# Seven block products in place of eight for the first product of layer 2, with that layer's weights staged through DRAM

## The chip, the cores and the metric

The program runs on one core of one Trainium2 chip. The metric is the device time of one execution in microseconds (us), as the median of three runs.

## The reference

Attention for 4 batches of 8 heads gives 2304 rows of 512. Two feed-forward layers follow, each with two matrix products around an activation:

```python
q_s, k_s = softmax(q, axis=-1), softmax(k, axis=2)      # 4 x 8 x 576 x 64
x = (q_s @ (k_s.T @ v)) laid out as 2304 x 512
h = x @ w_in1                   # 2304 x 2048
x = silu(h) @ w_out1            # 2304 x 512
h = x @ w_in2                   # 2304 x 2048
out = (h * tanh(softplus(h))) @ w_out2     # "mish"
```

All inputs and the output are float32.

## The kernel before, in words

Every float32 operand of the feed-forward products is split into a high part of TensorE's `float32r` type and a low part, the remainder. A product is then three products: high by high, high by low, low by high. The split costs a copy on ScalarE and a subtraction on VectorE. Before that, a weight is "decoded" (`w_take`, `w_join`), which is an activation on ScalarE and two or three bit operations on VectorE.

Activations lie transposed, 512 features in 4 groups of 128 partitions (`KC = 4`) by 2304 tokens. The 2048 hidden features are 16 chunks of 128 (`NCH = 16`). Each layer makes two passes (`passes`, p = 0 to 3) over 8 chunks each (`HALF = 8`). Pass 0 takes the tokens in six blocks of 384 (`NARROW`), the others in five blocks of 512, 512, 256, 512 and 512 (`WIDE`).

The order within a pass is the list `events`. `X` splits a token block. `G1` (`ev_g1`) makes one chunk of h: 12 matmuls of 128 by 128 weights with a token block as the moving side, into one PSUM bank, then the activation on ScalarE, and a cast and a subtraction on VectorE that split the result g. `G2` (`ev_g2`) is the second product with that chunk, three chunks later (`SKEW = 3`): 12 matmuls into four banks in layer 1, and in layer 2 three matmuls for each 128 tokens, with g as the stationary side and 512 columns of weights as the moving side. `E` (`ev_e`) adds up or copies out the four banks.

Pass 0 is woven with the attention, in an order that a scheduler makes from priorities. From the event where the attention's work is used up, all engines follow the written order: `InOrder` (line 49; calls before that are recorded at line 47). There the pools of the first part are closed and others are opened in the same memory, and `w_plan` sets the decoding of each later weight chunk at a time counted in events. A pass's 16 weight pieces are fetched from DRAM (`w_dma`, lines 156 and 161, three staging buffers `st`), decoded into `wt` and split into resident tiles (`w_high`, `w_low`) during the pass before it.

Of the kernel before, what the change touches and what calls it, by code (L numbers as in the profile page):

```python
# [7 lines left out]
F32 = mybir.dt.float32  # L8
# [24 lines left out]

class InOrder:
# [21 lines left out]
def attention_silu_mish(ctx: ExitStack, tc: tile.TileContext, q, k, v, w_in1, w_out1, w_in2, w_out2, out):  # L56
    nc = tc.nc
    SP = nc.sync
    V, S, G, T = (InOrder(tc, e) for e in (nc.vector, nc.scalar, nc.gpsimd, nc.tensor))
# [19 lines left out]
    PARTS = (((0, HALF), (HALF, NCH)),) * 2  # L79
# [21 lines left out]
    wres = ctx.enter_context(tc.tile_pool(name="wres", bufs=HALF))  # L101
# [6 lines left out]
    xa = xp.tile([P, KC * NT], F32, name="xa")  # L108
# [15 lines left out]

    passes = [(L, c0, c1) for L in range(2) for c0, c1 in PARTS[L]]
    blocks = [NARROW] + [WIDE] * (len(passes) - 1)
    events, need = [], []
    for p, (L, c0, c1) in enumerate(passes):
        cs = list(range(c0, c1))
        pend = []  # L130
        for j in range(len(blocks[p])):
            events.append(("X", p, j, 0))
            for c in cs:
                events.append(("G1", p, j, c))
                pend.append(("G2", p, j, c))
                if len(pend) > SKEW:
                    events.append(pend.pop(0))
            events.extend(pend)
            pend = []
# [10 lines left out]
    def w_dma():  # L150
        kind, p, _, c = need[state["dma"]]
        state["dma"] += 1
        L = passes[p][0]
# [12 lines left out]
    def at(i):  # L166

        tc.cur_priority = 10000 + int(1000 * i)

# [9 lines left out]
    def w_decode():  # L179
# [14 lines left out]
        w = wres.tile([P, 2, 512], F32R, tag="wi" if kind == "G1" else "wo", name="w")  # L194
# [23 lines left out]
    def w_plan(start):  # L218
        first_mish = next(i for i, e in enumerate(events) if e[1] == len(PARTS[0]))
        ends, taken, split = [], start, 0.0  # L220
        for n in range(N0, len(need)):
            kind, p, _, c = need[n]
            last = max(i for i, e in enumerate(events) if e == (kind, p - 1, len(blocks[p - 1]) - 1, c - HALF if c >= HALF else c + HALF))
            if n % N0 == 0:
                taken = max(taken, nat[("X", p - 1, 1, 0)])
# [6 lines left out]
            signed = b < first_mish - 1  # L232
            box = {}
            for k, f in ((b, w_take), (b + 1.0, w_join), (s, w_high), (s + 1.0, w_low)):
                todo.setdefault(int(k), []).append((k, f, n, signed, box))

    def w_take(n, signed, box):
# [4 lines left out]
        tf, hi = t.bitcast(F32), st[:, 1].bitcast(F32)  # L242
        if signed:
            S.activation(out=tf, in_=hi, func=ACTF.Prelu, scale=W_BIAS, alpha=W_SIGN)
            V.tensor_scalar(out=st[:, 0], in0=st[:, 0], scalar1=29, scalar2=None, op0=ALU.logical_shift_right)
        else:
            S.mul(tf, hi, W_BIAS)

    def w_join(n, signed, box):
        st, t = box["st"], box["t"]  # L250
        lo, hi = st[:, 0], st[:, 1]
        if signed:
            V.scalar_tensor_tensor(out=t, in0=t, scalar=3, in1=lo, op0=ALU.logical_shift_left, op1=ALU.bitwise_or)
        else:
            V.tensor_scalar(out=t, in0=t, scalar1=3, scalar2=None, op0=ALU.logical_shift_left)
            V.scalar_tensor_tensor(out=t, in0=hi, scalar=0x80000000, in1=t, op0=ALU.bitwise_and, op1=ALU.bitwise_or)
            V.scalar_tensor_tensor(out=t, in0=lo, scalar=29, in1=t, op0=ALU.logical_shift_right, op1=ALU.bitwise_or)

    def w_high(n, signed, box):
        kind, p, _, c = need[n]  # L260
        wt[(kind, p, c)] = w = wres.tile([P, 2, 512], F32R, tag="wi" if kind == "G1" else "wo", name="w")
        S.copy(w[:, 0], box["t"].bitcast(F32))

    def w_low(n, signed, box):
        kind, p, _, c = need[n]
        w = wt[(kind, p, c)]
# [558 lines left out]
```

## Time and profile before

| | before |
|---|---|
| median of 3 runs | 880.09 us (879.54 to 880.23) |
| the profiled execution: its time | 879.92 us |
| its span | 878.1 us |
| TensorE matmul (PE) busy | 860.3 us, 98% of the span |
| VectorE (DVE) busy | 437.2 us, 50% |
| ScalarE (ACT) busy | 296.7 us, 34% |
| moved by DMA | 53.17 MB, of it 4.72 MB written to HBM |

The span is what the profile covers; 1.8 us of the execution's time lie outside it. PE is the stream of matmuls, PEld the loads of stationary operands, which overlap it. A busy share does not tell what sets the end: for that the rows below show the chain of waits and stretches in order of time.

### The profile page before, as it was taken

What the parts mean: (1) busy time and instruction counts of PE and PEld (TensorE: products, weight loads), DVE (VectorE), ACT (ScalarE), POOL (GpSimd) and SP (SyncE); (2) the same over time, 40 slices, a digit from 0 to 9 for tenths busy, and PEclk for the clock granted to TensorE, in tenths of its full rate; (3) what the DMA queues carried; (4) which work ended last, traced back from release to release, by engine and by line L of the source; (5) the groups of instructions that cost most, each with busy time, mean ns of one, the idle gap of its engine ahead of it and who ended that gap; (6) DMA issues with size and microseconds to landing.
All of it is one profiled execution on the core that took longest, in us unless ns stands there. A gap on an engine that the chain in (4) does not pass through costs nothing.

```text
span 878.1 us, 11558 instructions
## 1 busy us (share of the span) xinstructions
PE 860.3 (98%) x4618; PEld 744.0 (85%) x4618; DVE 437.2 (50%) x904; ACT 296.7 (34%) x553; POOL 54.4 (6%) x82
## 2 busy tenths in 40 slices
PE   7899999999989999999999999999999999999998
PEld 6688989999989888898888888888888888888886
DVE  4999366773267634352357424463268433333332
ACT  5887254573155312121144222231144111121110
POOL 3145111231000000000000000000000000000000
PEclk9999999999999999999999999999999999999999
DMA  9996211310034401120013001130012010100101
GB/s 237 246 228 142 74 37 37 73 37 1 1 119 130 134 1 49 49 97 1 0 49 120 25 1 48 49 96 1 1 48 72 1 39 10 46 27 1 43 6 48
DMA packets 61909, 53.17 MB, mean 61 GB/s; under 512 B 30368, under 2 KB 55456, under 8 KB 61856
## 3 DMA queue, kind: packets, MB, share of 16 engines
q1 hardware_dynamic: 61856, 52.44, 21.3%
q8 instruction: 36, 0.59, 0.3%
q14 instruction: 17, 0.14, 0.1%
HBM read 47.71 MB, written 4.72 MB: 60 GB/s over the span
## 4 chain that ended last, share of the span: by engine, by line
PE 89%; DVE 5%; ACT 1%; DMA 1%; issue 1%; ACTq 0%; DVEq 0%; SPq 0%
PE psum L49 72%; PE psum L47 17%; DMA st<-in_moe_w_out_dram 1%; DVE g L47 1%; DVE qz L47 1%; DVE kmx L47 1%; DVE w L47 0%; DMA st<-in_moe_w_in_dram 0%; ACT xa L47 0%; DVE st L47 0%; DVE wt L47 0%; DVE xs L47 0%; DVE qmx L47 0%; DVE xs L49 0%; ACT xs L49 0%
## 5 line engine op out<-in xcount | busy, mean ns | idle before, releaser
L49 PE MATMUL psum<-xs,w 128*128 128x512 f32 (+2 forms) x1548 | 327.9, 366 | 1.8 <-ACT gf L49 1.8
L49 PEld LDWEIGHTS psum<-xs,w 128*128 128x128 f32 x1548 | 271.3, 189 | 47.7 <-ACT gf L49 2.1
L49 ACT ACTIVATE gf<-psum 128x512 f32<-128x512 f32 (+2 forms) x129 | 71.0, 550 | 407.5 <-PE psum L49 292.1
L49 PE MATMUL psum<-w,g 128*128 128x512 f32 x864 | 204.3, 390 | 0.0
L49 PEld LDWEIGHTS psum<-w,g 128*128 128x128 f32 x864 | 161.7, 188 | 33.0
L49 DVE CAST g<-gf 128x512 fp32r<-128x512 f32 (+2 forms) x129 | 51.3, 397 | 277.0 <-ACT gf L49 267.8
L49 PE MATMUL psum<-g,w 128*128 128x512 f32 (+2 forms) x624 | 128.8, 361 | 0.5 <-DVE g L49 0.5
L49 PEld LDWEIGHTS psum<-g,w 128*128 128x128 f32 x624 | 109.0, 188 | 15.8 <-DVE g L49 0.8
L47 PE MATMUL psum<-xs,w 128*128 128x384 f32 x468 | 98.4, 350 | 2.9 <-ACT gf L47 2.1
L47 PEld LDWEIGHTS psum<-xs,w 128*128 128x128 f32 x468 | 80.3, 189 | 7.1 <-ACT gf L47 3.2
L47 PE MATMUL psum<-g,w 128*128 128x384 f32 x432 | 84.7, 343 | 1.3 <-DVE g L47 1.3
L49 DVE TENSOR_TENSOR g<-gf,g 128x512 fp32r<-128x512 f32 (+2 forms) x129 | 81.7, 633 | 4.4
L47 PEld LDWEIGHTS psum<-g,w 128*128 128x128 f32 x432 | 74.7, 188 | 2.6 <-DVE g L47 1.8
L49 ACT CAST w<-wt 128x512 fp32r<-128x512 f32 x48 | 29.6, 617 | 23.0 <-DVE wt L49 14.6
L47 DVE CAST g<-gf 128x384 fp32r<-128x384 f32 x39 | 16.1, 413 | 38.9 <-ACT gf L47 38.6
L49 ACT ACTIVATE wt<-st 128x512 f32<-128x512 f32 x48 | 32.1, 670 | 4.5 <-DMA st<-in_moe_w_in_dram 4.5
L49 DVE TENSOR_TENSOR w<-wt,w 128x512 fp32r<-128x512 f32 x48 | 32.6, 685 | 0.5 <-ACT w L49 0.3
L47 ACT ACTIVATE gf<-psum 128x384 f32<-128x384 f32 x39 | 18.9, 490 | 40.9 <-PE psum L47 36.9
L47 ACT ACT_TABLE_LOAD x22 | 28.2, 1283 | 4.3 <-PE psum L47 2.4
L47 DVE TENSOR_TENSOR g<-gf,g 128x384 fp32r<-128x384 f32 x39 | 25.1, 644 | 1.0
L49 DVE TENSOR_TENSOR xa<-psum,xa 128x512 f32<-128x512 f32 x18 | 11.5, 686 | 27.5 <-PE psum L49 27.5
L49 DVE SCALAR_TENSOR_TENSOR wt<-st,wt 128x512 uint32<-128x512 uint32 x34 | 23.5, 692 | 1.2
(108 smaller groups left out, 546.7 us busy)
## 6 DMA issues: line engine op xcount, KB each, us to landing
st<-in_moe_w_in_dram SPq DMA_DIRECT2D x32, 512.0 KB, 3.8
st<-in_moe_w_out_dram SPq DMA_DIRECT2D x32, 512.0 KB, 3.4
out_dram<-xa SPq DMA_DIRECT2D x18, 256.0 KB, 2.1
xb<-in_k_dram SPq DMA_DIRECT2D x16, 144.0 KB, 3.4
xb<-in_v_dram SPq DMA_DIRECT2D x8, 288.0 KB, 6.9
xa<-in_k_dram SPq DMA_DIRECT2D x16, 144.0 KB, 6.4
xb<-in_v_dram SPq DMA_DIRECT2D x16, 144.0 KB, 3.7
qt<-in_q_dram SPq DMA_DIRECT2D x8, 192.0 KB, 3.3
```

The costliest lines, as they stand in the source:

```text
L47: return call(*args, **kwargs)
L49: self.last = call(*args, **kwargs)
```

## The change

The first product of layer 2 is done by Strassen's scheme in the Winograd form. A pair of chunks (2 x 128 hidden features) times a pair of token blocks (2 x 384 tokens), each side halved over the 512 input features too, makes a 2 by 2 block product. It takes 7 products of 256 features by 384 tokens, 42 matmuls (`prod`, 6 each), in place of 8. The layer's two passes become one sweep: 3 times 768 tokens (`NS`), in each of them 8 chunk pairs (`pair`, `NQ`), 24 pairs in all. Banks 0 to 5 hold the sums of the second product, so the seven products share one bank each for two running sums, `hs` (bank 6) and `hv` (bank 7). `keep` copies `hs` out between products, and `add` adds such a copy to `hv`. One queue of second products (`wait`) is served by `more`, 9 matmuls of 512 columns at a time: four times a pair, or three in the pairs of `FEWER`, and four times more after the first and second 768 tokens (`FLUSH`).

The token sums (`x2_sums`) are made on VectorE in the memory of the layer's input, and split by `x2_part`. The weights are decoded in layer 1 (`w_plan`), the sums of weight blocks are made there (`w_mix`), and all are written to DRAM (`q_store`, 7 stores for a pair). In the first 768 tokens they are read back (`q_load`, `o_load`), split (`q_split`, `o_split`), and the split form is written to DRAM as well; the second and third 768 tokens read the split form. In SBUF they lie in rings of 3 pairs and 5 chunks. In layer 1's second pass the cast of g moves from VectorE to ScalarE. SP's calls follow the written order as well.

At the switch to the written order the pools open in another sequence, three weight loads are issued ahead, and the plan starts 1.5 events later. The end, which before gathered the last four `G2` by token tile, now does so with what the queue still holds.

```diff
-    SP = nc.sync
-    V, S, G, T = (InOrder(tc, e) for e in (nc.vector, nc.scalar, nc.gpsimd, nc.tensor))
+    V, S, G, T, SP = (InOrder(tc, e) for e in (nc.vector, nc.scalar, nc.gpsimd, nc.tensor, nc.sync))
...
-    PARTS = (((0, HALF), (HALF, NCH)),) * 2
+    PARTS = ((0, HALF), (HALF, NCH))
...
+    NQ, NS, FEWER, FLUSH = NCH // 2, NT // (2 * BLK), (2, 3, 5, 6), 4
+    Q_PAIR, Q_RING, O_RING, O_AGE = 3584, 3, 5, 3
+    Q_END, Q_SHORT = 2.0, 0.3
...
-    wres = ctx.enter_context(tc.tile_pool(name="wres", bufs=HALF))
...
+    wall = wp.tile([P, 2 * HALF * 1024], F32R, name="wall")
+    wq = [dp.tile([P, Q_PAIR], F32, name=f"wq{i}") for i in range(NQ)]
+    wo = [dp.tile([P, 1024], F32, name=f"wo{i}") for i in range(NCH)]
+    wqf = [dp.tile([P, Q_PAIR // 2], F32, name=f"wqf{i}") for i in range(NQ)]
+    wof = [dp.tile([P, 512], F32, name=f"wof{i}") for i in range(NCH)]
...
+    events.pop()
+    for i in range(0, NCH, 2):
+        need += [("G1", 2, 0, i), ("G1", 2, 0, i + 1), ("G2", 2, 0, i), ("G2", 2, 0, i + 1)]
...
+        time = [0.0]
+        for e in events:
+            time.append(time[-1] + (1.0 if blocks[e[1]][e[2]][1] == 512 else Q_SHORT))
...
+        ev = (time[nat[("G1", 1, len(WIDE) - 1, HALF + 1)]] - Q_END - k) / (4 * NQ)
+        for q in range(NQ):
+            n = 2 * N0 + 4 * q
+            a, b, *cs = boxes = [{} for _ in range(4)]
+            for i, box in enumerate(boxes):
+                plan((when(k + ev * i), w_take, n + i, box), (when(k + ev * i) + 1.0, w_join, box))
+            mix = {}
+            h = when(k + ev) + 1.2
+            plan((when(k) + 1.4, q_store, a, "t", wqf[q][:, :512]), (h, w_mix, a, b, mix))
+            plan((h + 0.4, q_store, b, "t", wqf[q][:, 512:1024]), (h + 0.4, q_store, mix, "t", wqf[q][:, 1024:1536]))
+            plan((h + 0.4, q_store, mix, "z", wqf[q][:, 1536:]))
+            for i, box in enumerate(cs):
+                plan((when(k + ev * (2 + i)) + 1.4, q_store, box, "t", wof[2 * q + i]))
+            k += 4 * ev
...
-        if signed:
-            S.activation(out=tf, in_=hi, func=ACTF.Prelu, scale=W_BIAS, alpha=W_SIGN)
-            V.tensor_scalar(out=st[:, 0], in0=st[:, 0], scalar1=29, scalar2=None, op0=ALU.logical_shift_right)
-        else:
-            S.mul(tf, hi, W_BIAS)
-    def w_join(n, signed, box):
+        S.activation(out=t.bitcast(F32), in_=st[:, 1].bitcast(F32), func=ACTF.Prelu, scale=W_BIAS, alpha=W_SIGN)
+        V.tensor_scalar(out=st[:, 0], in0=st[:, 0], scalar1=29, scalar2=None, op0=ALU.logical_shift_right)
...
+    def w_mix(a, b, mix):
+        a, b = (t["t"].bitcast(F32).rearrange("p (l n) -> p l n", l=2) for t in (a, b))
+        u, z = (pools["tm"].tile([P, 512], U32, tag="wt", name="wt") for _ in range(2))
+        mix["t"], mix["z"] = u, z
+        u, z = (t.bitcast(F32).rearrange("p (l n) -> p l n", l=2) for t in (u, z))
+        V.tensor_tensor(out=u[:, 0], in0=b[:, 0], in1=b[:, 1], op=ALU.add)
+        V.tensor_tensor(out=u[:, 1], in0=u[:, 0], in1=a[:, 0], op=ALU.subtract)
+        V.tensor_tensor(out=b[:, 0], in0=a[:, 0], in1=b[:, 0], op=ALU.subtract)
+        V.tensor_tensor(out=z[:, 0], in0=a[:, 1], in1=u[:, 1], op=ALU.subtract)
+    def q_store(box, what, to):
+        t = box[what].bitcast(F32)
+        SP.dma_start(to, t[:, :to.shape[1]])
...
+        S.activation(out=gf, in_=h, func=ACTF.Silu)
+        (S.copy if p else V.tensor_copy)(g[:, 0], gf)
...
+    A11, A12, S3, A22, S1, S2, S4 = ((u, i * 2 * P) for u, i in ((0, 0), (0, 1), (1, 0), (1, 1), (2, 0), (2, 1), (3, 0)))
+    B11, B21, T2, T1, T3, T4, B22 = range(7)
...
+            V.tensor_tensor(out=t1, in0=b12, in1=b11, op=ALU.subtract)
+            yield
+            V.tensor_tensor(out=t2, in0=b22, in1=t1, op=ALU.subtract)
+            yield
+            V.tensor_tensor(out=t4, in0=b21, in1=t2, op=ALU.subtract)
+            yield
+            V.tensor_tensor(out=b12, in0=b22, in1=b12, op=ALU.subtract)
...
+    def x2_part(s, m):
+        for k in range(2):
+            t = sums.pop((s, m, k))
+            S.copy(x2[m][:, k, 0], t)
+            V.tensor_tensor(out=x2[m][:, k, 1], in0=t, in1=x2[m][:, k, 0].bitcast(F32), op=ALU.subtract)
...
+    def q_load(k):
+        if k < NQ:
+            for u in range(4):
+                w = q_unit(k, u)[:, 1].bitcast(F32)
+                SP.dma_start(w, wqf[k][:, u * 512:u * 512 + w.shape[1]])
+        elif k < NS * NQ:
+            SP.dma_start(wall[:, k % Q_RING * Q_PAIR:(k % Q_RING + 1) * Q_PAIR].bitcast(F32), wq[k % NQ])
+    def split(w):
+        S.copy(w[:, 0], w[:, 1].bitcast(F32))
+        V.tensor_tensor(out=w[:, 1], in0=w[:, 1].bitcast(F32), in1=w[:, 0].bitcast(F32), op=ALU.subtract)
+    def q_split(k, *units):
+        if k < NQ:
+            for u in units:
+                split(q_unit(k, u))
+            if 3 in units:
+                SP.dma_start(wq[k], wall[:, k % Q_RING * Q_PAIR:(k % Q_RING + 1) * Q_PAIR].bitcast(F32))
+    def o_slot(m):
+        at = Q_RING * Q_PAIR + m % O_RING * 1024
+        return wall[:, at:at + 1024]
+    def o_load(m, age=0):
+        if m < NCH:
+            SP.dma_start(o_slot(m)[:, 512:].bitcast(F32), wof[m])
+            loaded.append([m, age])
+        elif m < NS * NCH:
+            SP.dma_start(o_slot(m).bitcast(F32), wo[m % NCH])
+    def o_split():
+        for z in loaded:
+            z[1] += 1
+        if loaded and loaded[0][1] > O_AGE:
+            m, _ = loaded.pop(0)
+            split(o_slot(m).rearrange("p (i n) -> p i n", i=2))
+            SP.dma_start(wo[m], o_slot(m).bitcast(F32))
...
+    def prod(k, a, m, ps, first):
+        u, col = a
+        n = 256 if u == 3 else 512
+        for j, (iw, ix) in enumerate(((0, 0), (0, 1), (1, 0))):
+            for kc in range(2):
+                at = k % Q_RING * Q_PAIR + u * 1024 + iw * n + col + kc * P
+                T.matmul(ps, wall[:, at:at + P], x2[m][:, kc, ix], start=first and j + kc == 0, stop=j + kc == 3, skip_group_check=not first)
...
+    def act(s, c, b, h, gf):
+        i = turn2["g"] = (turn2["g"] + 1) % (8 + SKEW + 1)
+        pool = pools["g2"] if i < 8 else pools["g"]
+        g = pool.tile([P, 2, BLK], F32R, tag="g", name="g")
+        S.activation(out=gf, in_=h, func=ACTF.Mish)
...
+        g2[(s, c, b)] = g
+        wait.append((s, c, b))
...
+    def out_tile(s, b, n):
+        o = pools["ox"].tile([P, DM], F32, tag="ox", name="ox")
+        a = psum[:, (3 * b + n) * 512:(3 * b + n + 1) * 512]
+        if n % 2:
+            V.tensor_copy(o, a)
+        else:
+            S.copy(o, a)
+        it = (2 * s + b) * (BLK // P) + n
+        SP.dma_start(out[it * P:(it + 1) * P, :], o)
+    def second(s, c, b, n):
+        m = s * NCH + c
+        w = o_slot(m).rearrange("p (i n) -> p i n", i=2)
+        g = g2[(s, c, b)]
+        a = psum[:, (3 * b + n) * 512:(3 * b + n + 1) * 512]
+        i = done[(s, b, n)] = done.get((s, b, n), 0) + 1
+        for j, (iw, ig) in enumerate(((0, 0), (0, 1), (1, 0))):
+            T.matmul(a, g[:, ig, n * P:(n + 1) * P], w[:, iw], start=i == 1 and j == 0, stop=i == NCH and j == 2)
...
+    def more():
+        o_split()
+        if not wait:
+            return
+        s, c, b = wait.pop(0)
+        if s is None:
+            ev_g2(1, len(WIDE) - 1, c)
+            if c == NCH - 1:
+                ev_e(1, len(WIDE) - 1)
+            o_load(c - HALF - 3)
+            return
+        for n in range(BLK // P):
+            second(s, c, b, n)
+        if done[(s, b, 0)] == NCH:
+            for n in range(BLK // P):
+                out_tile(s, b, n)
+        k = used[(s, c)] = used.get((s, c), 0) + 1
+        if k == 2:
+            o_load(s * NCH + c + O_RING)
...
+        def keep():
+            t = f32("sc")
+            S.copy(t, hs)
+            return t
+        def add(t):
+            f = f32("hf")
+            V.tensor_tensor(out=f, in0=hv, in1=t, op=ALU.add)
+            return f
+        if q == NQ - 3 and s + 1 < NS:
+            x2_s[s + 1] = x2_sums(s + 1)
+        def part(m):
+            if last:
+                x2_part(s + 1, m)
+            elif m in (B11, T2, T1, T4) and q in (NQ - 3, NQ - 2) and s + 1 < NS:
+                next(x2_s[s + 1], None)
...
+        prod(k, A11, B11, hs, True)
+        s1 = keep()
+        prod(k, A12, B21, hv, True)
+        f = add(s1)
+        act(s, c, 0, f, f)
+        if k == 0:
+            x2_part(0, B22)
+        part(B11)
+        part(B21)
+        q_split(k + 1, 0, 1)
+        if q not in FEWER:
+            more()
+        prod(k, S2, T2, hs, False)
+        s2 = keep()
+        part(T2)
+        prod(k, S1, T1, hv, True)
+        more()
+        prod(k, S3, T3, hs, False)
+        s3 = keep()
+        f = add(s3)
+        act(s, c + 1, 1, f, f)
+        part(T1)
+        q_split(k + 1, 2, 3)
+        more()
+        prod(k, A22, T4, hs, False)
+        act(s, c + 1, 0, hs, f32("hf"))
+        prod(k, S4, B22, hv, False)
+        f = add(s2)
+        act(s, c, 1, f, f)
+        part(T3)
+        part(T4)
+        part(B22)
+        q_load(k + Q_RING)
+        more()
...
-            for nm, nb in (("xs", 1), ("gf", 2), ("g", SKEW + 1), ("st", 3), ("tm", W_WAIT)):
-                pools[nm] = ctx.enter_context(tc.tile_pool(name="l" + nm, bufs=nb, reuse_waits="tile"))
-            w_plan(i + 0.5)
...
+            for nm, nb in (("g", SKEW + 1), ("xs", 1), ("gf", 2), ("st", 3), ("tm", W_WAIT)):
+                into = ctx if nm == "g" else l1
+                pools[nm] = into.enter_context(tc.tile_pool(name="l" + nm, bufs=nb, reuse_waits="tile"))
+            for _ in range(3):
+                w_dma()
+            w_plan(i + 2.0)
...
+        if (what, p, j) == ("G1", 1, len(WIDE) - 1):
+            n = c - HALF
...
+                    list(x2_sums(0))
...
+                for m in ((), (), (), (B11, B21), (T2, T1), (T3, T4), (), ())[n]:
+                    x2_part(0, m)
+            if n in (3, 6, 7):
+                q_load((3, 6, 7).index(n))
+            if n > 5:
+                q_split(0, 2 * n - 12, 2 * n - 11)
+        if (what, p, j) == ("G2", 1, len(WIDE) - 1) and c - HALF in (3, 4):
+            o_load(c - HALF - 3, O_AGE - 1)
...
+    wait += [(None, c, None) for c in range(NCH - SKEW, NCH)]
+    for s in range(NS):
+        for q in range(NQ):
+            at(len(events) + 8 * (s * NQ + q))
+            pair(s, q)
+        if s + 1 < NS:
+            for _ in range(FLUSH):
+                more()
+    for b in range(2):
+        for n in range(BLK // P):
+            for s, c, bb in wait:
+                if bb == b:
+                    second(s, c, b, n)
+            out_tile(NS - 1, b, n)
```

## Rows read from the trace of the kernel before

**Rows 1.** The chain that ended last, from 250 us on: start, us, what.
```profile
249.69 3.81 DMA st<-in_moe_w_in_dram
...
254.63 619.74 PE psum L49 x2952
...
874.37 0.02 issue
```
**Rows 2.** Timeline of PE in pass 3 and pass 2: start, us, operation, number.
```profile
677.62 11.04 PE L49 MATMUL psum<-xs,w 128*128 128x512 f32 x48
688.50 1.75 PE L49 MATMUL psum<-w,g 128*128 128x512 f32 x7
```
**Rows 3.** The same in the 256-token block of pass 2.
```profile
568.08 5.92 PE L49 MATMUL psum<-xs,w 128*128 128x256 f32 x48
573.83 1.55 PE L49 MATMUL psum<-w,g 128*128 128x512 f32 x6
```
**Rows 4.** Timeline of PE around the switch to the written order, blocks of 384.
```profile
239.36 6.41 PE L49 MATMUL psum<-g,w 128*128 128x384 f32 x36
246.27 2.36 PE L49 MATMUL psum<-g,w 128*128 128x384 f32 x12 [0.51 <-DVE g L49]
248.47 4.33 PE L49 MATMUL psum<-xs,w 128*128 128x384 f32 x24
254.63 4.43 PE L49 MATMUL psum<-xs,w 128*128 128x384 f32 x24 [1.83 <-ACT gf L49]
258.89 2.24 PE L49 MATMUL psum<-g,w 128*128 128x384 f32 x12
260.98 2.24 PE L49 MATMUL psum<-xs,w 128*128 128x384 f32 x12
```
**Rows 5.** Timeline of DVE and ACT there.
```profile
245.86 0.36 DVE L49 CAST g<-gf 128x384 fp32r<-128x384 f32 x1 [8.94 <-PE psum L49]
253.53 0.68 ACT L49 ACTIVATE wt<-st 128x512 f32<-128x512 f32 x1 [4.51 <-DMA st<-in_moe_w_in_dram]
```
**Rows 6.** Timeline in pass 3: a chunk's hand-over from engine to engine.
```profile
847.00 2.88 PE L49 MATMUL psum<-w,g 128*128 128x512 f32 x12
847.24 0.60 ACT L49 ACTIVATE gf<-psum 128x512 f32<-128x512 f32 x1 [4.84 <-PE psum L49]
847.87 0.43 DVE L49 CAST g<-gf 128x512 fp32r<-128x512 f32 x1 [4.29 <-ACT gf L49]
```
**Rows 7.** Groups by shape, 160 to 410 us: busy, mean ns of one | idle before.
```profile
L49 ACT ACTIVATE gf<-psum 128x384 f32<-128x384 f32 x9 | 4.4, 488 | 16.5 <-PE psum L49 15.0 <-issue 1.1 <-ACT wt L49 0.5
L49 ACT COPY xb<-psum 128x384 f32<-128x384 f32 x4 | 1.7, 482 | 2.7 <-PE psum L49 2.7
L49 ACT CAST xs<-xa 128x384 fp32r<-128x384 f32 x4 | 1.7, 514 | 0.0
L49 ACT CAST w<-wt 128x512 fp32r<-128x512 f32 x16 | 9.8, 616 | 4.0 <-DVE wt L49 3.5 <-PE psum L49 0.5
L49 ACT ACTIVATE wt<-st 128x512 f32<-128x512 f32 x24 | 16.0, 670 | 4.5 <-DMA st<-in_moe_w_in_dram 4.5
L49 DVE CAST g<-gf 128x384 fp32r<-128x384 f32 x9 | 3.2, 359 | 14.8 <-PE psum L49 8.9 <-ACT gf L49 5.8
L49 DVE TENSOR_TENSOR g<-gf,g 128x384 fp32r<-128x384 f32 x9 | 5.0, 558 | 0.3
L49 DVE TENSOR_TENSOR w<-wt,w 128x512 fp32r<-128x512 f32 x16 | 11.0, 685 | 0.3 <-ACT w L49 0.3
L49 DVE SCALAR_TENSOR_TENSOR wt<-wt,st 128x512 uint32<-128x512 uint32 x24 | 16.5, 687 | 0.5
L49 DVE TENSOR_SCALAR st<-st 128x512 uint32<-128x512 uint32 x24 | 10.1, 423 | 0.9 <-DMA st<-in_moe_w_in_dram 0.9
L49 DVE TENSOR_TENSOR xs<-xa,xs 128x256 fp32r<-128x256 f32 x4 | 1.4, 419 | 0.0
```
**Rows 8.** Stretches: length, busy PE, PEld, DVE, ACT, POOL, clock, DMA share, GB/s.
```profile
0.00:30.00 30.00, 24.34 (x211) 19.76 (x212) 18.32 (x47) 19.73 (x38) 7.75 (x18) 1.00 0.89 233
30.00:60.00 30.00, 26.26 (x190) 22.83 (x190) 29.35 (x69) 25.69 (x46) 10.17 (x12) 1.00 1.11 255
283.86:294.78 10.92, 10.92 (x50) 9.02 (x50) 8.12 (x17) 5.78 (x11) 0.00 (x0) 1.00 0.49 157
```
**Rows 9.** Timeline of the end.
```profile
863.32 11.04 PE L49 MATMUL psum<-w,g 128*128 128x512 f32 x48
874.39 0.69 DVE L49 TENSOR_TENSOR xa<-psum,xa 128x512 f32<-128x512 f32 x1 [2.03 <-PE psum L49]
```

More of the change, by code (lines that the diff above doesn't have):

```diff
@@ L122, in attention_silu_mish @@
     xaO = xa.rearrange("p (i e) -> p i e", e=DM)
-    passes = [(L, c0, c1) for L in range(2) for c0, c1 in PARTS[L]]
-    blocks = [NARROW] + [WIDE] * (len(passes) - 1)
+    passes = PARTS
+    blocks = (NARROW, WIDE)
     events, need = [], []
-    for p, (L, c0, c1) in enumerate(passes):
+    for p, (c0, c1) in enumerate(passes):
         cs = list(range(c0, c1))
@@ L218, in w_plan @@
     def w_plan(start):
-        first_mish = next(i for i, e in enumerate(events) if e[1] == len(PARTS[0]))
         ends, taken, split = [], start, 0.0
-        for n in range(N0, len(need)):
+        for n in range(N0, 2 * N0):
             kind, p, _, c = need[n]
-            last = max(i for i, e in enumerate(events) if e == (kind, p - 1, len(blocks[p - 1]) - 1, c - HALF if c >= HALF else c + HALF))
-            if n % N0 == 0:
-                taken = max(taken, nat[("X", p - 1, 1, 0)])
+            last = max(i for i, e in enumerate(events) if e == (kind, p - 1, len(blocks[p - 1]) - 1, c - HALF))
             b = max(taken, ends[-W_WAIT] + 0.5 if len(ends) >= W_WAIT else 0.0)
@@ L670, in ev_g2 @@
     def ev_g2(p, j, c, tiles=None):
[L671 removed]
+        c0, c1 = passes[p]
         w = w_get("G2", p, c)
         g = gt[(p, j, c)]
+        n = blocks[p][j][1]
         if c == c0:
[L675 removed]
+            acc[(p, j)] = [banks("acc", (0, 1, 2, 3)) for _ in range(KC)]
         st, sp = (c == c0), (c == c1 - 1)
[L677 removed]
+        for k, (iw, ig) in enumerate(((0, 0), (0, 1), (1, 0))):
@@ L678, in ev_g2 @@
             for i, a in enumerate(acc[(p, j)]):
-                if tiles is not None and i not in tiles:
-                    continue
-                s = slice(i * P, (i + 1) * P)
-                if L == 0:
-                    T.matmul(a[:, :blocks[p][j][1]], w[:, iw, s], g[:, ig], start=st and n == 0, stop=sp and n == 2)
-                else:
-                    T.matmul(a, g[:, ig, s], w[:, iw], start=st and n == 0, stop=sp and n == 2)
-    def ev_e(p, j, tiles=None):
-        L, c0, c1 = passes[p]
+                T.matmul(a[:, :n], w[:, iw, i * P:(i + 1) * P], g[:, ig], start=st and k == 0, stop=sp and k == 2)
@@ new lines, in attention_silu_mish, with pair, f32 @@
+    used = {}
+    def pair(s, q):
+        k = s * NQ + q
+        c = 2 * q
+        last = q == NQ - 1 and s + 1 < NS
+        hs, hv = psum[:, 6 * 512:6 * 512 + BLK], psum[:, 7 * 512:7 * 512 + BLK]
+        def f32(tag):
+            return pools[tag].tile([P, BLK], F32, tag=tag, name=tag)
+        def keep():
[47 more added lines that the diff above has]
+        more()
@@ L775, in attention_silu_mish @@
         at(i)
-        if i >= len(events) - SKEW - 2:
-            if what == "G2":
-                tail.append(c)
-                continue
-            for n in range(blocks[p][j][1] // P):
-                for c in tail:
-                    ev_g2(p, j, c, (n,))
-                ev_e(p, j, (n,))
-            continue
         if what == "E":
```

128 lines of the change are left out of this document (74 added, 54 removed).

## Prediction

> **What bounds the kernel now.** I read the chain of waits first. From 254.6 us to the last evacuation it is one piece of TensorE matmuls, 619.7 us without a break [rows 1]. So in pass 1 and in all of layer 2 the end is set by the sum of the matmuls' own times, and every matmul saved there is saved at the end, as long as the stream stays unbroken. Only before that, at the switch to the written order, does a transfer stand in the chain [rows 1].
>
> Then I took the price of a matmul from the timeline of PE, start to start, since the listed durations overlap. 48 matmuls of 512 columns lie between 677.62 and 688.50: 226.7 ns each [rows 2]. 48 of 256 columns take 5.75 us: 119.8 ns [rows 3]. For 384 columns, 12 take 258.89 to 260.98, 2.09 us: about 174 ns; the straight line through the other two prices (107 ns for 256 columns, so 12.9 ns and 0.418 ns a column) gives 173.3, which I use [rows 2 to 4]. A matmul thus costs its columns and 13 ns.
>
> VectorE and ScalarE are busy 8.1 and 5.8 of 10.9 us in a full stretch after the switch [rows 8], and less on the whole; their rows [rows 7] price the new work. The granted clock is 1.00 there [rows 8].
>
> **The products.** Layer 2's G1 before: 16 chunks, 12 matmuls, over four blocks of 512 and one of 256: 768 x 226.7 + 192 x 119.8 ns = 174.1 + 23.0 = 197.1 us. After: 24 pairs of 42 matmuls of 384 columns, 1008 x 173.3 ns = 174.7 us. The second product is 864 matmuls of 512 columns before (16 chunks, 18 token tiles, 3) and after: 195.8 us both times. **Term: -22.4 us.** In columns the saving is an eighth; the narrower block takes back 0.6 us in the fixed 13 ns.
>
> The Trainium skill has a rule against this (TensorE: Matmul & The Clock Gate, Back-to-back issue gap): in a stream of weight loads and matmuls it gives about 81 ns at 128 columns and 131 at 512, so most of the price would be fixed. By that rule 384 columns cost 114 ns and 256 cost 98, and the sum would be 119.4 us before and 115.2 after, a saving of only 4 us. The trace disagrees: 226.7 ns at 512 columns [rows 2].
>
> **The seven products' two banks.** This is the new wait: each product ends in `hs` or `hv`, and the next use of that bank needs its copy or sum. A product is 6 x 173.3 ns = 1.04 us, a `more` 9 x 226.7 = 2.04 us. Where no `more` stands between (pairs 2, 3, 5, 6 of each eight) the third product would start 1.04 us after the first one ended. ACT starts 0.24 us after the last matmul, DVE 0.03 us after ACT [rows 6], and a copy of 384 from PSUM takes 0.48 us [rows 7]: 0.72 of 1.04 us. The fourth waits for the sum into `hv`, 1.04 us after the second: 0.24 + 0.55 us (a VectorE sum of 384, by the 558 ns subtraction [rows 7]) = 0.79. Margins of 0.32 and 0.25 us; at every other hand-over a `more` lies between, and the margin is over 1 us. That holds if ACT and DVE come to the copy at once, so their load counts.
>
> ACT per pair: 3 copies and 4 activations, 3 x 0.482 + 4 x 0.488 = 3.4 us. In the first 768 tokens the splits add 3 x 0.616 + about 0.4, and 2 x 0.616: 6.9 us in all. In the last pair of eight, 14 casts of 0.514: 10.6 us. DVE: 3 x 0.55 + 4 x (0.359 + 0.558) = 5.3; with the splits 3 x 0.685 + 0.419 + 2 x 0.685, 9.1; in the last pair 14 x 0.55 more, 13.1 [rows 7]. A pair lasts 7 x 1.04 + 3 or 4 x 2.04 = 13.4 or 15.4 us, and behind the last pair stand four `more` without products, 8.2 us. Nothing is over its time, and in the tight pairs no split stands between the first product and its copy. Cost taken: 0. If the margins are gone, 12 tight pairs pay up to the whole hand-over twice: 12 x 2 x 0.75 = 18 us, the upper bound; half of it, 9 us, for an engine that is late half the time.
>
> **The load on layer 1.** 32 pieces are decoded in pass 1 in place of 16. PE needs there 768 x 226.7 + 192 x 119.8 ns for each half of the two products, 197 us in all, and some 150 us of it, to the second chunk of the last block, are left after pass 1's own pieces: 4.7 us for a piece. ACT 0.67 and DVE 0.423 + 0.687, and four half-width sums of 0.419 for every four pieces [rows 7]: with a chunk's own work (5.4 us: ACT 0.6 + 0.62, DVE 0.69) no engine is half busy. SP, now in the written order too, waits there for VectorE before each store, and behind it stand the loads of pieces to come; those are asked for two pieces, 9 us, ahead, against 3.8 us for a load [rows 1]. The token sums and splits of layer 2's first tokens lie in the last block, where g has three chunks (16 us) of slack. Cost 0. The Mish table load delays the first activation of pair 0, which has four `more`, three of them of 12 matmuls: 0.
>
> **The switch.** Today PE stands 0.51 us there behind a cast of g, and 1.83 us behind an activation [rows 4]. The cast waited 8.94 us for PE, since the new g tiles lie over tiles of the old pool that were still read; ACT then waited 4.51 us for a weight load [rows 5] that was issued only when VectorE, so held up, had freed a staging buffer. In the new sequence g comes first in memory, over the old block's split tokens, which are free before the burst of G2 begins; the split of the next block then waits, but has that burst to do so. The plan begins 1.5 events later, so activations come ahead of the waiting decode. **Term: -2.3 us**; bounds 0 and -2.8 (48 matmuls of G2 from 239.36 to 248.47 took 9.1 us where 8.3 do, and the next 24 took 6.2 before the following start where 4.2 do [rows 4]).
>
> **The DMA queue in the first 768 tokens.** Per pair: raw weights 0.92 MB and 2 x 0.26 read, split ones 1.84 and 2 x 0.52 written: 4.33 MB in 13.4 us is 323 GB/s. Over the sweep, what must be through before the second 768 tokens is 7 x 0.92 + 8 x 1.84 + 16 x 0.26 + 16 x 0.52 + the first split set (1.84 + 1.05) = 36.6 MB, in 8 x 14.4 + 8.2 us and the 8.2 us before in which the second pair's weights are fetched, 131.7 us: 278 GB/s. Later sweeps need 200. The trace has 157 GB/s at a share of 0.49, so 320 at a full one; the most that it carried is 255 over 30 us, with small packets and the queue full [rows 8]. Rows of 2 to 14 KB, as here, should do at least 320, and a load has over a pair of lead, so I take no stall; the other bound is 255 GB/s: 36.6 / 0.255 = 143.5 us, +11.8. SP issues some nine DMAs a pair, in the order in which they can start.
>
> Does DMA slow the matmuls? At 157 GB/s 48 matmuls took 10.92 us [rows 8], against 10.88 in a quiet stretch [rows 2]: 0.4%. Twice that over the first 123 us and 0.4% over 247 would be 1.9 us. **Term: +1.0**, bounds 0 and 2.
>
> **The end.** Before, a VectorE sum (0.69 us) [rows 9], after, a ScalarE copy of some 0.6: -0.1. The queue's last seven entries, 63 matmuls, are in the sum, and the last g is ready before its turn.
>
> **Sum:** 879.9 (the profiled execution; the median is 0.2 above) - 22.4 - 2.3 + 1.0 - 0.1 = 856.1, by the median 856.3; I say 856.
>
> **Rivals.**
> 1. The queue carries only what it did at the start, 255 GB/s: loads come late in the first sweep, 856 + 11.8 = 868. For: the traffic is far beyond any stretch after 60 us, and large stores to DRAM are not in the trace. Against: that queue carried small packets [rows 8]. 17%.
> 2. Banks: copies or sums late in the tight pairs, 865 (bound 874). For: margins of a third of a us. Against: ACT and DVE are free at those points. 8%.
> 3. The fixed cost grows: each product is a short group of six that waits for another engine, and its first matmul pays what a restart costs. After the 0.51 us gap 12 matmuls took 2.20 us, 0.12 more than the price [rows 4]; 168 products x 0.12 = 20 us, 876. The skill's rule named above, with its large fixed part, leads to the same side. Against: groups of 12, which wait for other engines too, cost no more each than 48 in a row [rows 2, 4]. 2%.
> 4. Slower: the queue, with stores and loads of the same DRAM against each other, carries less than 235 GB/s. Then 36.6 MB take over 156 us, 24 more than there are, and the gain is gone; at the 233 of the first 30 us [rows 8] it is 157 us, 881. From 225 on it is measurably slower. 8%, and 3% that it ends within 0.2%.
> 5. That the saved matmuls were not on the path: excluded by the unbroken chain [rows 1].
>
> My forecast has the remaining 62%, with a range of its own of 853.5 to 860 (the switch from 0 to -2.8, contention from 0 to 2, a few small stalls). To leave out no more than 2 in 10 the range goes to 868.5, over the first rival and most of the second. A difference of 0.2% (1.8 us) is about what can be told from none here. Faster: 62 + 17 + 8 + 2 = 89%; same 3%; slower 8%.
>
> **What the profile after would show.** Right: 1008 matmuls of 384 columns with 173 ns from start to start, PE without a break from the switch to the end, layer 2 some 370 us long; ACT's and DVE's waits on PE, never PE's on them. Wrong: PE waiting for `wall` behind a DMA in the first 768 tokens (rival 1 or 4, the three stretches of 123 us unequal); PE waiting for `sc` or `hf` in pairs 2, 3, 5, 6 (rival 2); equal stretches, all long (rival 3); PE waiting for g in pass 1 would upset the load on layer 1, and a wait at 240 to 255 us the switch.

## The result, and the profile after

The changed kernel takes 860.76 us (median of 4 runs, 860.41 to 862.39) against 880.16 (4 runs, 879.54 to 882.29): a ratio of 0.9779, 95% interval 0.9758 to 0.98. The forecast of 856 had the sign and the range (853.5 to 868.5), but the gain was 19.4 us and not 24. The profiled execution was the slowest of the four, 862.39, with 3.3 us of it outside its span; so what follows goes by the spans, 878.1 and 859.1: 19.0 us less.

From the page: the DRAM traffic, and the two products of layer 2 by their groups (busy time, mean ns of one, idle time before).
```profile
HBM read 105.38 MB, written 39.32 MB: 168 GB/s over the span
...
L59 PE MATMUL psum<-wall,g 128*128 128x512 f32 x864 | 210.1, 390 | 0.0
L59 PE MATMUL psum<-x,wall 128*128 128x384 f32 x1008 | 191.8, 338 | 0.0
```
Both groups have 0.0 us of idle time before them. The traffic has almost trebled, from 53 to 145 MB; a run further down shows that PE does not feel it.

The chain of waits, its end (start, length), which answers to [rows 1]:
```profile
323.91 6.32 DMA st<-in_moe_w_in_dram
...
331.52 155.92 PE psum L59 x786
487.45 367.91 PE psum L59 x1830
855.43 0.59 ACT ox L59
```
From 331.52 on it is PE alone, as before. But a weight load stands in it now, in pass 1; the chain before had none after 254.6 us.

The timeline of PE at the switch and at that load (start, length), against [rows 4], and ScalarE's instruction on the piece that was loaded:
```profile
240.26 8.48 PE L59 MATMUL psum<-g,wall 128*128 128x384 f32 x48
248.58 8.48 PE L59 MATMUL psum<-xs,wall 128*128 128x384 f32 x48
...
281.86 11.08 PE L59 MATMUL psum<-xs,wall 128*128 128x512 f32 x48
...
325.42 5.60 PE L59 MATMUL psum<-xs,wall 128*128 128x512 f32 x24
331.52 5.76 PE L59 MATMUL psum<-xs,wall 128*128 128x512 f32 x24 [0.50 <-ACT gf L59]
337.12 2.88 PE L59 MATMUL psum<-g,wall 128*128 128x512 f32 x12
...
330.31 0.69 ACT L59 ACTIVATE wt<-st 128x512 f32<-128x512 f32 x1 [4.78 <-DMA st<-in_moe_w_in_dram]
```
Both stops at the switch are gone: 48 matmuls of G2 take 240.26 to 248.58, 8.32 us or 173.3 ns each, where the burst took 9.1 us. From the start of that burst to the start of pass 1 there are 41.60 us; before it was 239.36 to 283.86, 44.50. In pass 1 PE waits once, 0.50 us, and 48 matmuls take 325.42 to 337.12, 11.70 us, where an unbroken block takes 10.9.

Landmarks in PE's order split the 19.0 us. The start of the burst, which closes the first part, lies 0.9 us later (+0.9). The stretch up to pass 1 is 2.9 shorter. From there to the last evacuation it was 590.53 us (283.86 to 874.39) and is 573.57 (281.86 to 855.43): 17.0 shorter. +0.9 - 2.9 - 17.0 = -19.0, and the forecast's shortfall lies in the last stretch, which by the products' term should have given 22.4.

Next the price of a matmul there. The timeline of PE over a tight pair of the second 768 tokens:
```profile
643.88 4.40 PE L59 MATMUL psum<-x,wall 128*128 128x384 f32 x24
648.12 2.20 PE L59 MATMUL psum<-wall,g 128*128 128x512 f32 x9
650.16 1.22 PE L59 MATMUL psum<-x,wall 128*128 128x384 f32 x6
...
653.26 2.29 PE L59 MATMUL psum<-x,wall 128*128 128x384 f32 x12
655.38 2.24 PE L59 MATMUL psum<-wall,g 128*128 128x512 f32 x9
657.47 2.28 PE L59 MATMUL psum<-x,wall 128*128 128x384 f32 x12
```
Start to start, 24 product matmuls take 643.88 to 648.12, 4.24 us: **176.7 ns each, where 173.3 was forecast.** A `more` takes 2.04 us, nine times 226.7 ns, except the one behind the seventh product (655.38 to 657.47): 2.09. Over layer 2 that is 1008 x 3.4 ns = 3.4 us and 24 x 0.05 = 1.2 us. With 0.8 us for the stop in pass 1 these are the missing 5.4 us. In this pair PE is unbroken: nothing waits, each matmul of a product is a little longer.

The hand-over of the two banks in that pair, on the other engines (in brackets the wait before an instruction and its releaser):
```profile
645.14 0.48 ACT L59 COPY sc<-psum 128x384 f32<-128x384 f32 x1 [1.58 <-PE psum L59]
646.27 0.56 DVE L59 TENSOR_TENSOR hf<-psum,sc 128x384 f32<-128x384 f32 x1 [1.73 <-PE psum L59]
```
The first product ends at 644.94 (643.88 + 1.06), the copy at 645.62, and the third product starts at 646.00: a margin of 0.38 us. The sum ends at 646.83, the fourth starts at 647.06: 0.23. The forecast had 0.32 and 0.25.

Last the queue, by stretches of the first two sweeps over 768 tokens (length, busy PE, PEld, DVE, ACT, POOL, clock, DMA share, GB/s), and PE at the start of the second and the third sweep; the first starts at 471.70:
```profile
471.70:595.40 123.70, 123.69 (x618) 112.03 (x617) 80.40 (x162) 56.68 (x117) 0.00 (x0) 1.00 0.82 300
595.40:718.90 123.50, 123.50 (x619) 112.20 (x618) 53.47 (x112) 35.63 (x74) 0.00 (x0) 1.00 0.57 206
```
```profile
599.04 2.28 PE L59 MATMUL psum<-x,wall 128*128 128x384 f32 x12
...
724.05 2.28 PE L59 MATMUL psum<-x,wall 128*128 128x384 f32 x12
```
300 GB/s at a share of 0.82 in the first stretch, and PE busy throughout.

### The profile page after: what moved, and what is told of

The parts are those of the page before. It is cut to its first block, busy times and chain, and to the rows that moved or that the text cites. A ratio compares the mean times of both kernels' runs of the same rounds, so it can differ in the third digit from the quotient of the medians.

```text
span 859.1 us, 12311 instructions
## 1 busy us (share of the span) xinstructions
PE 842.5 (98%) x4666; PEld 755.1 (88%) x4666; DVE 467.4 (54%) x1004; ACT 364.6 (42%) x702; POOL 54.3 (6%) x82
## 4 chain that ended last, share of the span: by engine, by line
PE 87%; DVE 5%; DMA 3%; ACT 2%; SPq 1%; issue 1%; ACTq 0%; DVEq 0%
PE psum L59 70%; PE psum L57 17%; DMA st<-in_moe_w_in_dram 2%; SPq L57 1%; DMA st<-in_moe_w_out_dram 1%; DVE g L57 1%; DVE qz L57 1%; DVE kmx L57 1%; DVE wall L57 0%; ACT xa L57 0%; DVE wt L59 0%; DVE st L57 0%; DVE xs L59 0%; DVE wt L57 0%; DVE xs L57 0%
## 5 line engine op out<-in xcount | busy, mean ns | idle before, releaser
L59 PE MATMUL psum<-wall,g 128*128 128x512 f32 x864 | 210.1, 390 | 0.0
L59 PE MATMUL psum<-x,wall 128*128 128x384 f32 x1008 | 191.8, 338 | 0.0
L59 PEld LDWEIGHTS psum<-wall,g 128*128 128x128 f32 x864 | 161.3, 188 | 28.5 <-DVE xb L59 0.3
L59 PEld LDWEIGHTS psum<-x,wall 128*128 128x128 f32 x1008 | 179.9, 187 | 6.8
L59 PE MATMUL psum<-g,wall 128*128 128x512 f32 (+2 forms) x624 | 129.0, 360 | 0.0
L59 PE MATMUL psum<-xs,wall 128*128 128x512 f32 (+2 forms) x588 | 122.7, 362 | 0.5 <-ACT gf L59 0.5
L59 PEld LDWEIGHTS psum<-g,wall 128*128 128x128 f32 x624 | 109.0, 188 | 14.7
L59 PEld LDWEIGHTS psum<-xs,wall 128*128 128x128 f32 x588 | 102.7, 188 | 15.8 <-ACT gf L59 0.9
L57 PE MATMUL psum<-xs,wall 128*128 128x384 f32 x468 | 98.3, 350 | 2.7 <-ACT gf L57 1.9
L57 PEld LDWEIGHTS psum<-xs,wall 128*128 128x128 f32 x468 | 80.3, 189 | 6.8 <-ACT gf L57 2.8
L57 PE MATMUL psum<-g,wall 128*128 128x384 f32 x432 | 84.8, 343 | 1.3 <-DVE g L57 1.3
L57 PEld LDWEIGHTS psum<-g,wall 128*128 128x128 f32 x432 | 74.7, 188 | 2.7 <-DVE g L57 1.8
```

Of the source, the lines that this page charges most:

```text
L57: return call(*args, **kwargs)
L59: self.last = call(*args, **kwargs)
```

## The experiments

All but the first are the changed kernel or the kernel before with one edit or two. Ratios are to the kernel before on the same chip, with their 95% intervals. The first question was what makes a matmul 3.4 ns longer: the place of its operands in SBUF, the on-chip memory that holds the tiles (theory A), the short groups that follow other engines (B), or the DMA traffic (C).

**The changed kernel again.**

> The changed kernel again, as the yardstick for the other runs of this chip: 860.5 to 861.0 us. All theories expect the same here.

860.02 us, 0.9769 (0.975 to 0.9789). The timeline has the stop again, a little smaller, at `333.36`:
```profile
284.02 11.08 PE L59 MATMUL psum<-xs,wall 128*128 128x512 f32 x48
...
333.36 5.74 PE L59 MATMUL psum<-xs,wall 128*128 128x512 f32 x24 [0.17 <-ACT gf L59]
```
So it belongs to the kernel. This run is also the scatter against which the next ones are read: with the same program, pass 1 starts at 284.02 here and at 281.86 above, 2.2 us apart. In the other variants of the changed kernel it starts between 280.03 and 282.29. Differences of a us or so in a run's time are therefore read from its spacing, not from its total.

**Six of the seven token tiles of layer 2 moved down by 192 bytes.**
```diff
                         x2[m] = x2p.tile([P, 2, 2, BLK], F32R, name=f"x2{m}")
+                    x2p.tile([P, 48], F32, name="x2pad")
```


> The split token sums of the products B11 to T4 lie 192 bytes lower in SBUF, nothing else is changed. Theory A (the 176.7 ns of a product's matmul, where 173.3 were forecast, come from where its moving operand lies): the start-to-start time of these matmuls changes, back to 173.3 if this distance undoes it, and the time falls by up to 864 x 3.4 ns = 2.9 us, to some 858. Theory B (they come from products being short groups of six that each wait for another engine) and theory C (they come from the DMA traffic): 176.7 ns as before, no change within 0.3 us.

861.55 us, 0.9785 (0.9768 to 0.9803). The timeline of PE, the same pair, then its four products from the seventh and from the nineteenth matmul on:
```profile
643.48 4.38 PE L59 MATMUL psum<-x,wall 128*128 128x384 f32 x24
647.70 2.24 PE L59 MATMUL psum<-wall,g 128*128 128x512 f32 x9
649.78 1.23 PE L59 MATMUL psum<-x,wall 128*128 128x384 f32 x6
```
```profile
644.55 1.20 PE L59 MATMUL psum<-x,wall 128*128 128x384 f32 x6
...
646.63 1.05 PE L59 MATMUL psum<-x,wall 128*128 128x384 f32 x5
```
A move of 192 bytes changes the spacing, with nothing else altered. The 12 matmuls in the middle, 644.55 to 646.63, take 2.08 us: 173.3 ns each, the price that was forecast. But the six on either side, next to a `more`, take 1.07 us, more than the 1.06 of the changed kernel, and every `more` takes 2.08 us in place of 2.04, though its own operands did not move. So the place decides the price of a product's matmul, and with this place the change from products to second products and back costs something, which in the changed kernel it does only behind the seventh product. The sum does not fall. Theory A has the cause right and the size wrong.

**No traffic after the first sweep.** This kernel leaves out the stores of the split weights and all weight loads for the second and third 768 tokens, which then work with what the rings still hold.
```diff
-        elif k < NS * NQ:
-            SP.dma_start(wall[:, ...].bitcast(F32), wq[k % NQ])
...
-                SP.dma_start(wq[k], wall[:, ...].bitcast(F32))
...
-        elif m < NS * NCH:
-            SP.dma_start(o_slot(m).bitcast(F32), wo[m % NCH])
...
-            SP.dma_start(wo[m], o_slot(m).bitcast(F32))
```


> Leaves out the writing of split weights to DRAM and all loads of weights for the second and third 768 tokens, so these use whatever the rings still hold. Theory C (DMA traffic slows TensorE: the 3.4 ns, or the 1.1 us that the matmuls of 512 columns in layer 2 lost, or both): the second and third sweep fall to 173.3 and 226.7 ns, a gain of 0.7 us for the 512s alone and 3.0 with the 384s. Theories A and B: both stay as they were, 860.5 to 861.0 us. If the first sweep were held up by the queue, that would show as a gain too.

860.75 us, 0.9776 (0.9759 to 0.9793). The second sweep's stretch, then the timeline of PE:
```profile
595.00:718.00 123.00, 123.00 (x617) 111.78 (x616) 53.41 (x112) 35.63 (x74) 0.00 (x0) 1.00 0.04 14
```
```profile
643.02 4.40 PE L59 MATMUL psum<-x,wall 128*128 128x384 f32 x24
647.26 2.20 PE L59 MATMUL psum<-wall,g 128*128 128x512 f32 x9
```
With 14 GB/s in place of 206 the 24 matmuls take the same 4.24 us, and the `more` the same 2.04. Theory C falls.

**Four staging buffers in place of three.**
```diff
-            for nm, nb in (("g", SKEW + 1), ("xs", 1), ("gf", 2), ("st", 3), ("tm", W_WAIT)):
+            for nm, nb in (("g", SKEW + 1), ("xs", 1), ("gf", 2), ("st", 4), ("tm", W_WAIT)):
...
-            for _ in range(3):
+            for _ in range(4):
...
-        while state["dma"] < min(n + 3, len(need)):
+        while state["dma"] < min(n + 4, len(need)):
```


> Four staging buffers for raw weights in place of three after the switch, and loads asked for three pieces ahead in place of two. If the 0.5 us of PE's wait at 331.5 us, and the 0.66 us lost around it, come from a weight load that was issued too late, it goes, and the time is 0.6 to 0.9 us shorter: about 860.0. The rival, that VectorE and ScalarE have too much to do at that block's start: the wait stays, no change.

860.22 us, 0.9771 (0.9753 to 0.979). The timeline of PE at the place of the stop, and the stretch of those 48 matmuls by engine:
```profile
324.24 11.04 PE L59 MATMUL psum<-xs,wall 128*128 128x512 f32 x48
335.12 2.88 PE L59 MATMUL psum<-g,wall 128*128 128x512 f32 x12
```
```profile
324.24:335.12 10.88, 10.88 (x49) 9.01 (x48) 8.37 (x18) 4.81 (x8) 0.00 (x0) 1.00 0.97 324
```
48 matmuls in 10.88 us: the stop is gone, so the late load was its cause. The time beside the run above (860.02) does not resolve the 0.8 us. The queue carries 324 GB/s just then, and the matmuls take what they took in the quiet stretch of [rows 2].

**Other distances.** The same tiles moved by 448 bytes (`x2p.tile([P, 112], ...)`), to test whether the place modulo 512 counts; everything else moved by 448 bytes in their stead (a gap tile ahead of the weights); and the first of these with four staging buffers.
```diff
     mask = const.tile([P, 2, D], F32, name="mask")
+    const.tile([P, 112], F32, name="cpad")
```


> The split token sums lie 448 bytes lower than in the changed kernel (the shift of 192 changed the products' matmuls and also those behind them). In the program all other operands of TensorE, weights and g, start at 32 bytes over a multiple of 512; the sums start at 480 over, after the shift of 192 at 288, after this one at 32 like the rest. Theory A2 (a matmul costs 173.3 and 226.7 ns when moving and stationary operands lie alike modulo 512 bytes): all matmuls of layer 2 go back to these, 4.8 us less than the changed kernel, about 855.5. Rival A3 (any distance from the old place shifts the cost about without a rule): a sum between 3 and 6 us stays. Rival B (groups of six): 384 columns stay at 175 to 177 ns.

> The reverse of the run before: the split token sums stay where they are, and a gap of 448 bytes ahead of the weights moves weights, g, layer 1's operands and the rest up, so that all lie at 480 over a multiple of 512. Theory A2, that the difference between the operands counts: the same gain, about 855.5. Rival, that each operand's own place against multiples of 512 counts: no gain, and layer 1's matmuls of 512 columns get slower as well, 1 to 3 us more than the changed kernel.

> The shift of 448 bytes and the four staging buffers together. If both causes are right and independent: 4.8 + 0.8 us less than the changed kernel, about 854.7.

860.98 us, 0.9788 (0.9768 to 0.9807); 860.69, 0.9779 (0.9763 to 0.9795); 862.08, 0.9792 (0.9776 to 0.9809). The timeline of PE with the sums moved by 448 bytes, then with all else moved:
```profile
640.71 2.24 PE L59 MATMUL psum<-wall,g 128*128 128x512 f32 x9
642.79 4.38 PE L59 MATMUL psum<-x,wall 128*128 128x384 f32 x24
647.01 2.24 PE L59 MATMUL psum<-wall,g 128*128 128x512 f32 x9
```
```profile
640.58 2.24 PE L59 MATMUL psum<-wall,g 128*128 128x512 f32 x9
642.66 4.38 PE L59 MATMUL psum<-x,wall 128*128 128x384 f32 x24
646.88 2.24 PE L59 MATMUL psum<-wall,g 128*128 128x512 f32 x9
```
Both show the spacing of the 192-byte move, to the digit (2.08 and 4.22 us). Whether the tokens or the weights move does not matter, so the place of one operand alone does not decide; how the two lie to each other does, as far as these runs go. The guess that all matmuls get cheap when the places agree modulo 512 bytes (A2) falls, and so does the third kernel, whose 854.7 never came. A shorter period is open: the two moves differ by 256 bytes and give the same spacing.

**An eighth product**: the first of each pair is made twice, so that the work of eight is done in the new structure.
```diff
         prod(k, A11, B11, hs, True)
+        prod(k, A11, B11, hs, True)
```


> The first product of each pair is made twice, 48 matmuls in place of 42, with the same output: the saving of the seven products undone in the new structure. If the end is set by the matmuls' sum, each of the 24 added products costs its 6 x 176.7 ns, 25.4 us: about 885.7, 6 us slower than the kernel before. If a product's time hid in waits for the two banks, it would cost less; if the second use of the bank waited for anything, more.

884.78 us, 1.0052 (1.0036 to 1.0068): 24.0 us over the changed kernel's 860.76, or 1.0 us for each of the 24 added products. In the trace, free of the first part's scatter, the second sweep takes 133.5 us (605.46 to 738.95) and not 125.0 (599.04 to 724.05): 1.06 us for each of its eight, which is their six matmuls. So the gain in layer 2 is the saving of seven for eight and nothing else, and the structure without it, the new switch included, is 0.5% slower than the kernel before.

**The kernel before, with the new switch alone.**
```diff
-            for nm, nb in (("xs", 1), ("gf", 2), ("g", SKEW + 1), ("st", 3), ("tm", W_WAIT)):
+            for nm, nb in (("g", SKEW + 1), ("xs", 1), ("gf", 2), ("st", 3), ("tm", W_WAIT)):
                 pools[nm] = ctx.enter_context(tc.tile_pool(name="l" + nm, bufs=nb, reuse_waits="tile"))
-            w_plan(i + 0.5)
+            for _ in range(3):
+                w_dma()
+            w_plan(i + 2.0)
```


> The kernel before with the edit at the switch alone: the pools open in the new sequence, three weight loads are issued ahead, the plan starts 1.5 events later. By the traces before and after, the stretch from the last G1 of the fifth block to the start of pass 1 fell from 46.58 to 43.68 us. If the switch does that by itself: 2.9 us less than the kernel before, 877.1 or so. Rival, that the shorter stretch comes from SP's written order or the single weight tile: no change.

877.08 us, 0.9961 (0.9947 to 0.9974). Its timeline of PE:
```profile
240.36 8.48 PE L49 MATMUL psum<-g,w 128*128 128x384 f32 x48
...
281.96 11.08 PE L49 MATMUL psum<-xs,w 128*128 128x512 f32 x48
```
41.60 us between the landmarks, the figure of the changed kernel, so the switch edit alone gives the 2.9 us.

**The same, with a gap of 64 bytes ahead of the split tokens.** If the operands' places are the cause, they must lengthen matmuls in the old kernel too, where products of 384 columns and second products do not alternate.
```diff
+                if nm == "xs":
+                    ctx.enter_context(tc.tile_pool(name="gap", bufs=1)).tile([P, 16], F32, name="gap")
```


> The run before with the split tokens of the feed-forward products (G1's moving operand) 64 bytes higher, from the switch on. The kernel before has no block products. Theory A (the distance of the moving operand, in steps of 64 bytes, sets the 3.4 ns): G1's matmuls rise by some 3.3 ns each, 384 + 96 in pass 1 and 768 + 192 in layer 2, 4.8 us in all, and G2's hardly change. Theory B2 (it takes blocks of different length behind each other, as products of 384 columns and second products of 512): only the blocks of 256 change, under 1 us.

883.21 us, 1.003 (1.0019 to 1.0042): 6.1 us more than without the gap, where theory A expected 4.8. The timeline of PE from the last burst of layer 1 on, without it, then with it:
```profile
468.26 11.04 PE L49 MATMUL psum<-g,w 128*128 128x512 f32 x48
479.14 11.04 PE L49 MATMUL psum<-xs,w 128*128 128x512 f32 x48
490.02 2.88 PE L49 MATMUL psum<-w,g 128*128 128x512 f32 x12
492.74 2.88 PE L49 MATMUL psum<-xs,w 128*128 128x512 f32 x12
```
```profile
469.32 11.09 PE L49 MATMUL psum<-g,w 128*128 128x512 f32 x48
480.25 11.17 PE L49 MATMUL psum<-xs,w 128*128 128x512 f32 x48
491.25 2.93 PE L49 MATMUL psum<-w,g 128*128 128x512 f32 x12
494.02 2.93 PE L49 MATMUL psum<-xs,w 128*128 128x512 f32 x12
```
48 matmuls of G1, whose tokens moved, take 11.00 us in place of 10.88. 48 of G2, none of whose operands moved, take 10.93, and 12 of G2 take 2.77 in place of 2.72: 0.05 us more in either, so a G2 group pays at the change from the other stream and not for each matmul. Theory A holds in that a place alone lengthens matmuls, and B2 falls as it was put, since not only the blocks of 256 change. But streams that follow each other count as well, and the kernel before pays for that with no gap: behind a block of 256 columns six matmuls of 512 go from 573.83 [rows 3] to 575.22, 1.39 us, where six times 226.7 ns are 1.36.
```profile
575.22 1.60 PE L49 MATMUL psum<-xs,w 128*128 128x256 f32 x12
```
The 6.1 us are more than expected, since the second product grew as well.

**The seventh token tile (`B22`) moved by 64 bytes, with four staging buffers.**
```diff
+        if nm == "x7":
+            ctx.enter_context(tc.tile_pool(name="gap", bufs=1)).tile([P, 16], F32, name="gap")
```


> The changed kernel with four staging buffers, and with the seventh product's sums (B22, which lie apart from the others) 64 bytes higher, so that they stand to the weights as the other six do. In the changed kernel the seventh product and the nine matmuls of 512 columns behind it are the only ones with irregular gaps, 68 ns together, where others have 20. Theory A: these go to the others' pattern, 24 x 48 ns = 1.1 us less, and with the stall at 331 us gone 0.7 more: about 858.5 to 859, the fastest version. Rival, that the end of a pair itself makes the gaps: only the stall's share.

859.21 us (858.37 to 860.5), 0.9759 (0.9743 to 0.9775), and a span of 856.2. The timeline of PE:
```profile
650.59 2.26 PE L59 MATMUL psum<-x,wall 128*128 128x384 f32 x12
652.69 2.23 PE L59 MATMUL psum<-wall,g 128*128 128x512 f32 x9
654.75 2.28 PE L59 MATMUL psum<-x,wall 128*128 128x384 f32 x12
```
The products before that `more` take 2.10 us (2.12 in the changed kernel), the `more` 2.06 (2.09). It is the lowest ratio of all, though its interval overlaps that of the changed kernel.

**All eight pairs tight** (`FEWER` is all of them, `FLUSH` 8). The longer queue leaves chunk 15's second products of the third sweep with chunk 10's weights.
```diff
-    NQ, NS, FEWER, FLUSH = NCH // 2, NT // (2 * BLK), (2, 3, 5, 6), 4
+    NQ, NS, FEWER, FLUSH = NCH // 2, NT // (2 * BLK), tuple(range(8)), 8
```


> All eight pairs of a sweep have three servings of second products in place of four in half of them, and eight behind the last pair in place of four: the same matmuls, but no cover between the first and third product in any of 24 pairs (12 before). If the margins of 0.32 and 0.25 us hold, PE stays unbroken and the time is that of the changed kernel within 0.5 us. If copies and sums are late, up to 0.75 us twice in each of 12 more pairs, 18 us.

860.23 us, 0.9772 (0.9755 to 0.9789). Of PE's waits in layer 2, grouped by what they are for (total us, times, longest), one is left:
```profile
PEld psum L59 <- DVE hf L59: 0.4, 1, 0.4
```
Twice the tight pairs cost nothing that can be measured: two banks suffice.

## Why the prediction was right, and where 4.8 us went

Spans are compared: forecast -23.8, measured -19.0.

- **The products, -22.4 forecast: the term that was mis-sized.** The step is "173.3, which I use": the straight line through the prices of 512 and 256 columns in the old kernel, carried over to the new one's products. Measured were 176.7 ns, so 178.1 us for the 1008 matmuls and not 174.7; and 197.0 for the second products, which "195.8 us both times" held unchanged. With these the term is -17.8. The line itself holds for 384 columns: 173.3 ns in the burst of pass 0, and in the middle products once the sums are moved. What it left out is that the price also hangs on where the operands lie and on which stream comes before. That a place moves prices by this much is shown by a 64-byte gap in the old kernel (+6.1 us) and by the moved sums in the new. Which places are cheap, and by what mechanism, is open: three moves gave one and the same worse sum, a fourth a slightly better one, and none brought all matmuls to the line's price. An estimate on the line through the two figures of the Trainium skill (TensorE: Matmul & The Clock Gate, Back-to-back issue gap) would put 384 columns at about 114 ns; the trace, with 176.7, disagrees again.
- **The load on layer 1, 0 forecast: +0.8.** The count of busy engines was right, but the lead was not enough: a load asked for "two pieces, 9 us, ahead" against 3.8 us was issued at 323.91, 1.6 us before ScalarE came to the piece, and took 6.3 us. ScalarE waited 4.78 us for it, and the activation `gf` that frees PE's bank stood behind. A fourth buffer removes the stop.
- **The switch, -2.3: -2.9**, shown alone by the old kernel with that edit; the upper bound had been 2.8.
- **The banks, 0: 0**, with margins of 0.38 and 0.23 us, and 0.4 us lost once when all pairs are tight. Rival 2 falls.
- **The queue, 0: 0.** It carried 300 GB/s; the second sweep (599.04 to 724.05, 125.0 us) and the first (127.3 with three of layer 1's 2.72 us groups where 2.04 us groups stand later, so 125.3) are equal but for 0.3 us, which PE loses at 487 us to VectorE's last sums of layer 1 and not to the queue. Rivals 1 and 4 fall.
- **DMA slowing the matmuls, +1.0: 0.** Without the traffic nothing gets shorter, and 48 matmuls take 10.88 us at 324 GB/s. The 10.92 us of [rows 8] from which the term was read belong to the first matmuls of 512 columns behind a block of 384: the first ten of them take 2.31 us, ten at the price 2.27, so the 0.04 us are a change of streams as above. So the term, which happened to soften the error, had no cause.
- **Fixed cost per product (rival 3).** All stretches were longer by a little, as it said, but not by a restart of 0.12 us for each product: an added product costs its six matmuls, 1.06 us. What is paid by groups is the 0.05 us behind each seventh product, 1.2 us in all and not 20.
- **The first part, not in the sum: +0.9.** The work there is the same. The burst starts at 240.26, in the old kernel with the new switch at 240.36, in the profile before at 239.36. The changed kernel run again comes to pass 1 2.2 us later than in its first profile, so 0.9 us lies within the scatter of that part; what scatters there is open.

Together: +5.4 in the last stretch, -0.6 at the switch, +0.9 ahead of it, -1.0 for the traffic and 0.1 at the end: 4.8 us.

## What to carry to other kernels

Where the path is an unbroken stream of matmuls, the forecast is only as good as the price of one, and a price read for operands in one place, behind one stream, need not hold in another place or behind another stream: give it a bound of some 2%, and after a change read the spacing start to start, for the middle of a group and its edges apart, since no wait will show it. To learn what a structure costs by itself, put the saved work back into it, as the eighth product did. A count of busy time does not cover loads: check each against its lead where two queues of work meet, as at the start of a token block.

## What the runs showed of the hardware that was not expected

- With the moving operand of one product 64 bytes higher in SBUF, 48 of its matmuls of 512 columns took 11.00 us and not 10.88, and the kernel 883.21 us and not 877.08. The other product's groups, whose operands had not moved, took 0.05 us more per group, whether of 12 matmuls or of 48.
- With the sums moved by 192 or 448 bytes, or all else by 448, products of 384 columns showed the same spacing: 173.3 ns between other products, and more next to second products.
- The DMA queue carried 300 GB/s of mixed loads and stores for 124 us at a share of 0.82, where the most in the old kernel's rows was 255 [rows 8]. TensorE's spacing was the same at 206 GB/s and at 14 (4.24 us for 24 matmuls), and 48 matmuls took 10.88 us at 324 GB/s.
